# Two attention-only slots, a gate weight spread by a transfer, and loads in another order, in a fused attention and mixture-of-experts kernel

## The chip, the cores and the metric

The kernel runs on one core of one Trainium2 chip. The metric is device time of one execution in microseconds (us), lower is better, taken without the profiler; where a profile is discussed, the span is that of one profiled execution. A run counts as slow when it is more than 1.5% above the fastest run of the same kernel in the same rounds, and only fast runs enter a ratio. In lines of a profile PE is TensorE, PEld its weight loads, DVE VectorE, ACT ScalarE, POOL GpSimd and SP SyncE; L596 is line 596 of that run's kernel. The granted clock is the share of full speed at which TensorE runs.

## The reference

Eight batches of windowed attention, each followed by one expert chosen for the whole batch.

```python
# attention: q, k, v are (8, 8, 576, 64); heads 0-3 a plain window of 32, heads 4-7 a dilated one of 128
scores = np.where(masks, scale * q @ k.T, -1e9)
attn = softmax(scores)                       # exp, row sum, divide
x = (attn @ v).transpose(0, 2, 1, 3).reshape(B, S, 512)
# mixture of experts, w1 (8, 512, 1024), w2 (8, 1024, 512)
logits = x.mean(axis=1) @ w_gate             # one row of 8 logits for each batch
e_idx = argmax(logits)                       # one expert for the whole batch
gate_w = softmax(logits)[e_idx]
out = gate_w * (relu(x @ w1[e_idx]) @ w2[e_idx])
```

Which expert's 2 MB are loaded is known only when the attention of the batch is complete.

## The kernel before

The attention of a batch is cut into four slots of two heads; slots 4b to 4b+3 belong to batch b, 32 slots in all. Queries and keys are transposed on TensorE, a group of two slots at a time and some slots ahead. A slot forms scores, takes the exponent (ScalarE), masks (VectorE), multiplies by v and by ones for the row sums, and normalises by way of a logarithm and an exponent. Between these steps stand items of the feed-forward network of the batch before: 16 of the first layer (four products and a ReLU each), four of the second layer, and a tail. `PIECES` says how many items stand in each slot.

```python
PIECES = [0] * 5 + [6, 3, 4, 4, 1, 1, 2] + [8, 8, 2, 3] * 7

def emit_gate(b):
    lg = ...                                    # gate product, 128x1 against 128x8, 4 chunks
    nc.vector.tensor_copy(out=l_sb[:], in_=lg)
    nc.vector.max_with_indices(mx[:], mi[:], l_sb[:])
    e_val = nc.values_load(mi[0:1, 0:1]..., engines=[ET.Pool], ...)
    # ... three (batch 0: six) loads of w1[e_val] ...
    if b == 0:
        load_1(2, GO[0], "q")                   # second half of batch 2's first group: queries
        load_va(2); load_qb(2); load_w2(e_val, w2b); load_qa(3); load_vb(2)
    else:
        load_vb(b + 2); load_w2(e_val, w2b); load_qa(b + 3)
    load_va(b + 3)
    load_qb(b + 3)

def emit_gate_bc(b):                            # gate weight to 128 partitions
    nc.tensor.matmul(bct[:, 0:1], lhsT=ones1[:], rhs=s["gw"][:], start=True, stop=True)
    nc.vector.tensor_copy(out=gbc[:], in_=bct[:, 0:1])

for t in range(5, len(PIECES)):
    # first half of a slot's items: ReLU on VectorE ("D"), second half on ScalarE ("A")
    # ... run_T (transposes), emit_gate, pre.av_a, cur.sx, pre.av_b, pre.ln, cur.mask, pre.rd,
    #     first half of the items, pre.norm, second half of the items ...
```

`load_qa` and `load_qb` load the queries and keys of a batch's first and second group of slots, `load_va` and `load_vb` the values. All of them and the expert's weights are issued by GpSimd, in program order, into one queue. An item that stands ahead of an attention step in an engine's program can hold it up: in the profile of this kernel VectorE normalised slot 4 at 37.38 us, behind three ReLUs, though ScalarE's reciprocal was ready at 31.76.

The softmax here doesn't subtract the row's maximum and nothing guards it: scores larger than these inputs give would overflow.

## Time and profile before

| | before |
|---|---|
| time, median of 3 | 225.6 us (224.1 to 226.86) |
| profiled span | 220.8 us |
| exponent of slot 4, 12, 31 starts at | 26.5, 67.0, 178.5 us |
| length of a steady batch (four slots) | 23.6 us |
| TensorE busy | 200.8 us, 91% |

I use the start of a slot's exponent on ScalarE as a milestone all through: it is one instruction per slot, easily found, and it stands between that slot's scores and its mask. From slot 4 to 12 is the early part (40.5 us here), from 12 to 31 the steady part (111.5), and after that comes the rest of the feed-forward (42.4). The profile is of a run of 221.91 us. The lines of the profile that carry the argument are shown inside the prediction.

### The profile page before, as it was taken

What the parts mean: (1) busy time and instruction counts of PE and PEld (TensorE: products, weight loads), DVE (VectorE), ACT (ScalarE), POOL (GpSimd) and SP (SyncE); (2) the same over time, 40 slices, a digit from 0 to 9 for tenths busy, and PEclk for the clock granted to TensorE, in tenths of its full rate; (3) what the DMA queues carried; (4) which work ended last, traced back from release to release, by engine and by line L of the source; (5) the groups of instructions that cost most, each with busy time, mean ns of one, the idle gap of its engine ahead of it and who ended that gap; (6) DMA issues with size and microseconds to landing.
All of it is one profiled execution on the core that took longest, in us unless ns stands there. A gap on an engine that the chain in (4) does not pass through costs nothing.

```text
span 220.8 us, 8308 instructions
## 1 busy us (share of the span) xinstructions
PE 200.8 (91%) x3598; PEld 136.0 (62%) x3598; DVE 129.3 (59%) x366; ACT 129.9 (59%) x229; POOL 83.1 (38%) x133
## 2 busy tenths in 40 slices
PE   6976848899889999999999999999999999999992
PEld 1564745675557765777567756776577657747641
DVE  6346644765777756765666766665676556415312
ACT  2368761786767776577656665766667754332320
POOL 7966095614835263525460455236103100500000
PEclk9975556999999999999999999999999999999999
DMA  5999979999999999999999999999995997499523
GB/s 81 182 177 181 97 100 163 207 209 162 207 214 234 216 207 196 245 255 207 199 235 232 213 208 222 219 230 211 218 193 134 190 176 228 50 174 259 117 95 119
DMA packets 49924, 41.18 MB, mean 187 GB/s; under 512 B 23776, under 2 KB 38112, under 8 KB 49888
## 3 DMA queue, kind: packets, MB, share of 16 engines
q0 software_dynamic: 43440, 31.20, 96.4%
q1 hardware_dynamic: 6448, 9.46, 12.7%
q8 instruction: 28, 0.46, 0.8%
q14 instruction: 8, 0.07, 0.1%
HBM read 62.41 MB, written 9.44 MB: 325 GB/s over the span
## 4 chain that ended last, share of the span: by engine, by line
PE 67%; ACT 12%; DVE 9%; DMA 6%; issue 2%; POOL 2%; POOLq 0%; SPq 0%
PE m L622 24%; PE m L602 22%; ACT pt L335 6%; PE nd L370 6%; PE m L637 4%; DMA qm<-in_q_dram 3%; DVE pt L342 3%; PE m L268 3%; DVE xt L507 3%; ACT qk L289 2%; PE m L278 2%; DMA w1b<-in_moe_w_dram 2%; PE ps L302 2%; DVE ht L609 2%; ACT rd L480 2%
## 5 line engine op out<-in xcount | busy, mean ns | idle before, releaser
L602 PE MATMUL m<-xt,w1b 128*128 128x288 bf16 x512 | 69.3, 291 | 5.2 <-DMA w1b<-in_moe_w_dram 3.0
L602 PEld LDWEIGHTS <-w1b 128*128 128x128 bf16 x512 | 49.3, 99 | 21.1 <-issue 4.5
L622 PE MATMUL m<-w2b,ht 128*128 128x512 bf16 x256 | 58.0, 380 | 0.0
L607 ACT ACTIVATE ht<-m 128x288 bf16<-128x288 f32 x63 | 25.8, 409 | 28.8 <-PE m L602 25.3
L622 PEld LDWEIGHTS <-ht 128*128 128x128 bf16 x256 | 23.8, 98 | 27.4
L342 DVE TENSOR_TENSOR pt<-pt,mk 128x896 bf16<-128x896 bf16 x32 | 20.0, 625 | 24.2 <-ACT pt L335 24.2
L507 DVE SCALAR_TENSOR_TENSOR xt<-nd,rd 128x320 bf16<-128x320 f32 (+1 forms) x56 | 28.4, 544 | 7.8 <-ACT rd L480 7.8
L609 DVE TENSOR_SCALAR ht<-m 128x288 bf16<-128x288 f32 x65 | 27.6, 453 | 7.8 <-PE m L602 7.2
L335 ACT ACTIVATE pt<-ps 128x896 bf16<-128x896 f32 x32 | 29.0, 906 | 5.3 <-PE ps L302 5.3
L543 POOL DMA_DIRECT2D w1b<-in_moe_w_dram x9 | 6.4, 708 | 58.9 <-PE m L602 29.6
L289 ACT ACTIVATE qk<-m 128x576 bf16<-128x576 bf16 (+1 forms) x26 | 19.0, 730 | 15.4 <-PE m L268 12.1
L137 POOL DMA_DIRECT2D vm<-in_v_dram x32 | 24.1, 765 | 8.2 <-DMA qm<-in_q_dram 3.0
L286 DVE COPY qk<-m 128x576 bf16<-128x576 bf16 (+1 forms) x26 | 20.4, 783 | 8.4 <-PE m L268 7.1
L480 ACT ACTIVATE rd<-lnd 128x576 f32<-128x576 f32 x32 | 21.8, 683 | 1.0
L370 PEld LDWEIGHTS <-vm 64*64 64x64 bf16 x896 | 15.4, 113 | 9.9 <-issue 3.7
L629 DVE TENSOR_SCALAR osb<-m,gbc 128x512 f32<-128x512 f32 x16 | 12.0, 750 | 15.6 <-PE m L622 15.6
L370 PE MATMUL nd<-pt,vm 64*64 64x64 bf16 (+2 forms) x784 | 18.1, 194 | 3.3 <-DVE negm L575 1.9
L474 ACT ACTIVATE lnd<-nd 128x576 f32<-128x576 f32 x28 | 18.0, 644 | 2.9 <-PE nd L370 2.9
L370 PE MATMUL nd<-pt,ones 64*64 64x256 bf16 (+2 forms) x252 | 16.5, 243 | 0.0
L627 ACT ACTIVATE osb<-m,gbc 128x512 f32<-128x512 f32 x16 | 10.9, 681 | 8.7 <-PE m L622 8.6
L302 PE MATMUL ps<-qk 64*64 64x96 bf16 (+3 forms) x608 | 15.0, 207 | 0.5 <-DVE mx L535 0.4
L302 PEld LDWEIGHTS <-qk 64*64 64x64 bf16 x608 | 14.2, 113 | 1.2 <-issue 0.7
(76 smaller groups left out, 210.5 us busy)
## 6 DMA issues: line engine op xcount, KB each, us to landing
w2b<-in_moe_w_dram POOLq DMA_DIRECT2D x8, 1024.0 KB, 12.6
out_dram<-osb SPq DMA_DIRECT2D x32, 256.0 KB, 6.2
km<-in_k_dram POOLq DMA_DIRECT2D x16, 288.0 KB, 11.9
qm<-in_q_dram POOLq DMA_DIRECT2D x16, 288.0 KB, 12.2
w1b<-in_moe_w_dram POOLq DMA_DIRECT2D x16, 256.0 KB, 10.1
w1b<-in_moe_w_dram POOLq DMA_DIRECT2D x7, 512.0 KB, 10.5
vm<-in_v_dram POOLq DMA_DIRECT2D x8, 256.0 KB, 10.4
vm<-in_v_dram POOLq DMA_DIRECT2D x32, 64.0 KB, 9.4
```

What stands on the lines that cost most here:

```text
L137: nc.gpsimd.dma_start(out=t[:, h], in_=v[b, h, 0:512, :].rearrange("(c p) d -> p c d", p=P))
L289: nc.scalar.activation(out=ev[x][0], in_=ev[x][1], func=AF.Copy)
L302: nc.tensor.matmul(ps[half(e), a, o : o + rhs.free_size()], lhsT=lhsT, rhs=rhs, start=True, stop=True, skip_group_check=True)
L335: nc.scalar.activation(out=pt[:], in_=s["ps"][:, :, 0:NP], func=AF.Exp, scale=0.125)
L342: nc.vector.tensor_tensor(out=pt[:], in0=pt[:], in1=mk[:, g : g + 1, :].to_broadcast([P, 2, NP]), op=ALU.mult)
L370: x = nc.tensor.matmul(oo, lhsT=lhsT, rhs=rhs, start=start, stop=True, skip_group_check=True)
L480: nc.scalar.activation(out=rd[:], in_=s["lnd", n][:], func=AF.Exp, scale=-1.0)
L507: nc.vector.scalar_tensor_tensor(out=o, in0=a0, scalar=1.0, in1=a1, op0=ALU.mult, op1=ALU.mult, accum_out=s["pool"][:, w, c : c + 1],)
L602: nc.tensor.matmul(hm, lhsT=s["w1"][:, c, fc * P : (fc + 1) * P], rhs=s["xt"][:, c, cols], start=(c == 0), stop=(c == 3))
L607: nc.scalar.activation(out=o, in_=hm, func=AF.Relu)
L609: nc.vector.tensor_scalar_max(out=o, in0=hm, scalar1=0.0)
L622: nc.tensor.matmul(om, lhsT=s["ht"][:, fc, r * P : (r + 1) * P], rhs=s["w2"][:, fc, :], start=(fc == 0), stop=(fc == 7))
```

## The change

The intent: slots 5 and 6 do not wait for the first expert's weights, because they hold attention only, with three products on dummy data each, meant to bring TensorE's full clock sooner; the product that spreads the gate weight gives way to a small transfer within the on-chip memory; the gate product moves from the middle of attention to a place beside feed-forward products; in each slot with much feed-forward the first item's product goes ahead of the logarithm, and its ReLU to ScalarE; and loads go in the order of need, with batch 2's queries ahead of the first gate.

```diff
-PIECES = [0] * 5 + [6, 3, 4, 4, 1, 1, 2] + [8, 8, 2, 3] * 7
+PIECES = [0] * 7 + [6, 6, 5, 2, 2] + [8, 8, 2, 3] * 7
...
-    load_1(2, GO[0], "k")
+    load_qk(2, GO[0])
...
-        nc.vector.tensor_copy(out=l_sb[:], in_=lg)
-        nc.vector.max_with_indices(mx[:], mi[:], l_sb[:])
+        nc.vector.max_with_indices(mx[:], mi[:], lg)
+        nc.vector.tensor_copy(out=l_sb[:], in_=lg)
...
-        if b == 0:
-            load_1(2, GO[0], "q")
-            ...
-        load_va(b + 3)
-        load_qb(b + 3)
+        load_va(b + 2)
+        load_qb(b + 2)
+        load_w2(e_val, w2b)
+        load_qa(b + 3)
+        load_vb(b + 2)
...
-        nc.tensor.matmul(bct[:, 0:1], lhsT=ones1[:], rhs=s["gw"][:], start=True, stop=True)
-        nc.vector.tensor_copy(out=gbc[:], in_=bct[:, 0:1])
+        nc.sync.dma_start(out=gbc[:], in_=gw[0:1, 0:1].to_broadcast([1, P]))
...
+        lead = n >= 5 and done % 21 < 16 and pre.on
+            e = "A" if (lead and i == 0) or 2 * i >= n else "D"
+        if gn == 0 and 0 < gb < B:
+            emit_gate(gb)
         if t > 5:
             run_T(t)
-        if gn == 0 and 0 < gb < B:
-            emit_gate(gb)
...
         pre.av_b()
+        if lead:
+            items.pop(0)()
         pre.ln()
...
+        if t in (5, 6):
+            busy_late(3, 512)
```

## The prediction

> **What bounds the kernel now.** I read the busy shares of the page first, then the chain that ended last, then a table of stages, then the timelines of the stages that stood out. The unprofiled time is 225.6 us; the profiled span is 220.8 us.

> From the page (busy time of each engine; the chain by engine and by line; the two DMA queues with packets, MB and share of 16 engines' span):

> ```profile
> PE 200.8 (91%) x3598; PEld 136.0 (62%) x3598; DVE 129.3 (59%) x366; ACT 129.9 (59%) x229; POOL 83.1 (38%) x133
> ...
> PE 67%; ACT 12%; DVE 9%; DMA 6%; issue 2%; POOL 2%; POOLq 0%; SPq 0%
> ...
> q0 software_dynamic: 43440, 31.20, 96.4%
> q1 hardware_dynamic: 6448, 9.46, 12.7%
> ```

> Two resources are nearly full: TensorE (91%, two thirds of the chain) and the transfer engines (the load queue alone 96.4%). So I ask of each stage which of the two is behind. The stage table (from:to and length in us, then busy time and instruction count of PE, weight load, DVE, ACT, POOL, then granted clock, DMA share, GB/s):

> ```profile
> 28.40:33.90 5.50, 2.49 (x92) 2.36 (x92) 1.60 (x5) 3.15 (x6) 5.50 (x9) 0.50 0.91 110
> 33.90:37.40 3.50, 3.48 (x15) 2.24 (x16) 1.31 (x4) 0.00 (x0) 0.80 (x3) 0.51 1.10 170
> 37.40:52.20 14.80, 13.57 (x297) 9.77 (x294) 10.52 (x31) 10.90 (x19) 6.49 (x10) 1.00 1.32 201
> 52.20:65.60 13.40, 11.57 (x281) 7.62 (x282) 9.00 (x24) 10.11 (x16) 7.74 (x12) 1.00 1.22 199
> 65.60:89.25 23.65, 23.32 (x452) 16.17 (x453) 16.02 (x48) 15.99 (x28) 11.34 (x18) 1.00 1.34 217
> 89.25:112.80 23.55, 23.14 (x450) 16.09 (x452) 15.62 (x44) 15.89 (x28) 10.64 (x17) 1.00 1.29 225
> ```

> TensorE idles 5.5-2.49 = 3.0 us in the first row, 1.2 in the third, 1.8 in the fourth, but only 0.33 and 0.41 us in each steady batch of 23.6 us. So the early part has 6 us of holes; later only removing work, or those 0.4 us, can pay.

> The chain in order of time (start, us, what) shows the early hole and one steady batch:

> ```profile
> 28.93 4.86 DMA w1b<-in_moe_w_dram
> 33.92 4.76 PE m L602 x24
> ...
> 95.19 0.68 PE m L268 x36
> 95.87 0.28 PE m L530 x8
> 96.14 0.39 PE nd L370 x19
> ...
> 101.42 0.31 PE m L589 x2
> ...
> 114.29 0.80 ACT pt L335
> 115.11 0.63 DVE pt L342
> 115.73 0.38 DVE ht L609
> 116.15 2.61 PE m L602 x20
> ```

> First pair: TensorE waits for the first expert's w1, behind which slot 5's attention has to queue, since its instructions come after the feed-forward in order. L268, L530, L370: transposes, gate product, attention. L589: the product that spreads the gate weight. The last four: softmax exponent, mask and the first ReLU on VectorE, and only then the next feed-forward product, because its three PSUM banks are full.

> [...] 0.50 is granted up to 37.35 us, 3.4 us after the feed-forward began at 33.92. [...] the gate product in mid attention: from transposes to attention takes 96.14-95.19 = 0.95 us with it and, in the slot before, 0.50 without it (timeline: 112.76 to 113.26), so it costs 0.45 where its own chain piece is 0.28. [...] packets of the load queue run without a break from 35 to 169 us, at about 210 GB/s for weights alone and half of that beside a burst of stores.

> **The change, part by part.**

> *Slots 5 and 6 without feed-forward.* Before, the normalisation of slot 4 could run when its reciprocal was ready (31.76 us) but started at 37.38, behind three ReLUs that waited for w1. After, it runs at once, and slot 6's attention can begin at about 33.1. An attention slot held up by its own chain has a period of 4.2 us (53.3 to 57.5 us in the timeline); with about 0.5 us for half clock slot 7 begins near 37.0 with its transposes. It then has 21 items in 5 slots: 16 of 0.52 (2.61/5), four of 1.78 (chain: 3.56 for two) and a tail of 0.99: 16.5 us. Five slots' own TensorE work is 1.5 each (5.95 us of an eight-item slot less 8 x 0.52 and the 0.3 us stall): 7.5. I add 1.2 for the clock (0 if the dummy products of slots 5 and 6 wake it early[...]) and 0.8 of residual stalls: 37.0+24.0+2.0 = 63.0, and 0.6 for the longer lead of ReLU and logarithm on ScalarE: 63.6, against 65.6. Gain 2.0 us.

> *Gate weight by a transfer.* The product goes from TensorE: 0.31 us, on the chain in each batch. Batch 0's is in the 2.0 above; seven remain: 2.2 us. The transfer is issued three slots before its first use from batch 1 on and two slots before in batch 0, some 10 us; the gate table's 4 KB landed in 4.7 us. It hides. It waits in SyncE's queue for the gate weight, behind which the attention fences stand, but the weight is ready a slot earlier.

> *One ReLU to ScalarE, with its product ahead of the logarithm.* The bank of that item is emptied without waiting for mask or VectorE, so the 0.29 us at 115.86 to 116.15 and its like go. At most the idle time of a batch, 0.4 us, in the five batches that overlap attention fully: 2.0 us.

> *Gate product next to feed-forward.* [...] 0.45-0.28 = 0.17 us, six batches: 1.0 us. The maximum read directly from PSUM brings the expert number about 0.8 us earlier, which only helps loads.

> *Load order.* No bytes change. Query load of batch 2 moves into the gap of 26 to 28.5 us in which the queue was empty: 1.5 us of transfer time won. The rest gives up prefetching 1.77 MB (4.3 us) per batch: w1 lands earlier, batch b+2's second half of keys later. Before, w1 packets of batches 2 to 5 began 23.0 to 23.6 us apart with the engines never idle: transfers can barely go faster than the old TensorE pace. With TensorE at about 22.6 us a batch it catches up. My reckoning of service times (w1 5.0, v 1.6, keys 1.5 us after the queue reaches w1) has the keys just in time in batches 1 to 3 and late by about 0.5 and 0.8 us in 4 and 5. Loss 1.3 us.

> Sum: 2.0+2.2+2.0+1.0-1.3 = 5.9 us; 225.6-5.9 = 219.7 us (2.6%).

> **Rivals.** (a) Transfers become the bound. For: 96.4%, and the never-empty queue. Against: 3.5 us between w1's landing and its use in a steady batch, and 5.0 us for w2 of batch 5. If the smaller prefetch leaves the queue empty at gates or keys late in each batch, gains after the start shrink to about 2 us: 222 to 223.5. (b) The early slots gain nothing: attention alone is bound by its ScalarE-VectorE chain and half clock, and the feed-forward merely moves later: 2 us lost, 221.5. (c) The dummies wake the clock at 37.35 as before and no key is late: 1.2+1.3 more, 217. (d) The spread transfer blocks the fences or lands late: up to 1 us a batch, 226. Against it: the slack above.

> **Range and chances.** (c) gives the low end, (a) the high end; 216.8 to 223.2 should hold it 8 times in 10. 2% is 4.5 us, that is 221.1; my centre is 1.4 us below this, with a spread of about 2.4: faster 0.72, same 0.26, slower 0.02.

> **What would show it.** The first feed-forward product near 39 to 40 us with no wait for w1; granted clock 1.00 from 37.4 (c), 40.8 or 44.2; the transposes of slot 12 near 63.6 instead of 65.6; no spread product in the chain; TensorE idle in a steady batch near 0; batch length about 22.7 instead of 23.6, unless transposes wait for keys, which is (a). If batch length stays at 23.6 the prediction is wrong in its second half; if slot 12 starts at 65 or later, in its first.

## The result, and the profile after

Ratios here and below are the mean time of one kernel's fast runs over that of the other's fast runs of the same rounds, so they are not quite the ratio of the medians quoted beside them.

| | before | after |
|---|---|---|
| first rounds, median | 226.23 us (224.1 to 228.09, 4 runs) | 217.78 us (216.42 to 218.44, 4 runs) |
| ratio, first rounds | | 0.9649, 95% interval 0.9552 to 0.9746: faster |
| later rounds, median | 226.91 us (221.75 to 229.32, 11 runs) | 219.1 us (217.03 to 219.51, 6 runs) |
| ratio, later rounds | | 0.9801, interval 0.9736 to 0.9866: unclear at 2% |
| profiled span | 220.8 us | 214.8 us |
| exponent of slot 4, 12, 31 | 26.5, 67.0, 178.5 us | 25.7, 64.5, 173.1 us |
| steady batches | 23.6, 23.6, 23.6, 23.9 us | 22.5, 22.5, 23.8, 23.1 us |

The medians agree in both rounds (217.78/226.23 = 0.963, 219.1/226.91 = 0.966). The ratios differ because the kernel before scatters: in the later rounds six of its eleven runs, from 226.91 to 229.32, count as slow, and the five fast ones average 223.12. In the first rounds, where the fastest run was 224.1, one of 226.86 still counted as fast. The changed kernel has no such group in ten runs. Among the fast runs of the later, larger rounds the change is worth 2%, in the medians over 3%. Why the kernel before scatters so I did not find out; its one profile is of a fast run. The mean granted clock goes with it (0.936 to 0.947 in its six slow runs of the later rounds, 0.949 to 0.954 in the five fast ones), but no trace shows what lowered it.

Busy times, queues and chain of the changed kernel's page:

```profile
PE 192.6 (90%) x3571; PEld 131.5 (61%) x3588; DVE 122.0 (57%) x343; ACT 133.6 (62%) x243; POOL 83.0 (39%) x133
...
q0 software_dynamic: 43440, 31.20, 97.6%
q1 hardware_dynamic: 7600, 9.46, 14.2%
q8 instruction: 28, 0.46, 0.8%
...
PE 50%; DMA 34%; issue 4%; POOL 4%; DVE 3%; ACT 2%; POOLq 0%; SPq 0%; DVEq 0%
```

The load queue's packets and megabytes are those of before, and its share rose from 96.4 to 97.6%, since the span shrank. The chain that ended last now runs through transfers for a third (6% before). "issue" doubled from 2 to 4%; I had not looked at it. The 28 packets of queue 8 were there before as well, and play a part below.

The stage table of the changed kernel (from:to and length, then busy time and count of PE, weight load, DVE, ACT, POOL, then clock, DMA share, GB/s):

```profile
27.60:32.20 4.60, 4.32 (x103) 3.31 (x103) 2.78 (x9) 3.16 (x6) 4.57 (x9) 0.56 0.95 117
32.20:36.50 4.30, 2.17 (x66) 1.71 (x67) 2.69 (x7) 3.44 (x5) 1.38 (x2) 1.00 1.10 163
...
40.50:47.20 6.70, 4.72 (x125) 3.68 (x124) 3.29 (x11) 4.71 (x9) 1.37 (x2) 1.00 1.24 210
...
63.10:85.60 22.50, 22.39 (x446) 15.79 (x448) 15.05 (x45) 16.52 (x30) 10.10 (x16) 1.00 1.28 221
85.60:108.10 22.50, 22.29 (x448) 15.76 (x450) 14.59 (x41) 16.55 (x30) 9.31 (x15) 1.00 1.29 223
108.10:131.90 23.80, 22.74 (x446) 15.79 (x446) 15.11 (x42) 16.37 (x30) 9.97 (x15) 1.00 1.27 216
```

Four readings. The clock is full from 31.67 us (37.35 before), ahead of the first feed-forward product. The hole before that product has become a hole in slot 7's attention, 4.30-2.17 = 2.1 us. A new hole stands at 40.5 to 47.2: TensorE is idle 2.0 us of 6.7, at full clock. The first two steady batches leave TensorE idle 0.11 and 0.21 us; the next one 1.06.

TensorE's timeline of the changed kernel from 36 us on, lines with long idle time ahead (in brackets: idle before, and what ended it), and the first feed-forward products:

```profile
36.50 0.34 PE L373 MATMUL nd<-pt,vm 64*64 64x64 bf16 x16 [1.97 <-DVE xt L510]
37.41 3.11 PE L596 MATMUL m<-xt,w1b 128*128 128x288 bf16 x24
...
42.91 0.33 PE L373 MATMUL nd<-pt,ones 64*64 64x256 bf16 x6 [1.54 <-issue]
...
49.10 0.23 PE L373 MATMUL nd<-pt,vm 64*64 64x64 bf16 x3 [0.71 <-issue]
...
120.09 0.68 PE L281 MATMUL m<-identb,km 128*128 128x128 bf16 x9 [0.32 <-DMA km<-in_k_dram]
...
131.91 0.69 PE L271 MATMUL m<-ident,km 64*64 64x64 bf16 x32 [0.51 <-DMA km<-in_k_dram]
...
139.26 0.26 PE L305 MATMUL ps<-qk 64*64 64x80 bf16 x6 [0.47 <-issue]
...
167.43 0.27 PE L373 MATMUL nd<-pt,vm 64*64 64x80 bf16 x8 [0.69 <-issue]
```

No wait for w1 is left: the first feed-forward product runs at 37.41. The attention of slot 7 waits 1.97 us for a normalisation, the price of attention alone. Two kinds of wait were not there before: keys that arrive late (120.09, 131.91), and pauses called "issue", in which TensorE waits for nothing that the profile shows. The kernel before has none of these over 0.25 us in its steady part.

The moved ReLU in ScalarE's timeline of the changed kernel (L601 is a ReLU, L477 the logarithm):

```profile
87.76 0.42 ACT L601 ACTIVATE ht<-m 128x288 bf16<-128x288 f32 x1
88.05 0.68 ACT L477 ACTIVATE lnd<-nd 128x576 f32<-128x576 f32 x1
```

And the spread transfer's own view of the changed kernel (issue time in ns; landing time in us, min/median/max):

```profile
L585 SPq DMA_DIRECT2D gbc<-gw x8: 513/524/557, 37.1 to 191.8; - x8
...
DMA to landing us min/median/max: 5.8/7.8/8.8
```

Nothing waited for it; it took 7.8 us, and the first use of its result came 12.5 to 19.9 us after its issue.

By milestones the profiles differ by 0.8 us at slot 4, 2.5 at slot 12, 5.3 at slot 31 and 6.0 at the end. The first 0.8 is luck: slot 4 begins anywhere from 25.4 to 26.9 us in the runs, for kernels alike up to there; why it varies was not tested. That leaves 1.7 for the early part, 2.8 for the steady one and 0.7 for the rest.

### The profile page after: what moved, and what is told of

It reads as the page before. It is cut to its first block, busy times and chain, and to the rows that moved or that the text cites. A ratio compares the mean times of both kernels' runs of the same rounds, so it can differ in the third digit from the quotient of the medians.

```text
span 214.8 us, 8277 instructions
## 1 busy us (share of the span) xinstructions
PE 192.6 (90%) x3571; PEld 131.5 (61%) x3588; DVE 122.0 (57%) x343; ACT 133.6 (62%) x243; POOL 83.0 (39%) x133
## 3 DMA queue, kind: packets, MB, share of 16 engines
q0 software_dynamic: 43440, 31.20, 97.6%
q1 hardware_dynamic: 7600, 9.46, 14.2%
## 4 chain that ended last, share of the span: by engine, by line
PE 50%; DMA 34%; issue 4%; POOL 4%; DVE 3%; ACT 2%; POOLq 0%; SPq 0%; DVEq 0%
DMA qm<-in_q_dram 19%; PE m L596 19%; PE m L616 15%; DMA w2b<-in_moe_w_dram 8%; PE nd L373 5%; DMA km<-in_k_dram 4%; DMA w1b<-in_moe_w_dram 3%; PE m L271 3%; PE ps L305 2%; PE m L631 2%; PE e L373 1%; DVE xt L510 1%; PE m L281 1%; POOL vm L144 1%; POOL km L129 1%
## 5 line engine op out<-in xcount | busy, mean ns | idle before, releaser
L596 PE MATMUL m<-xt,w1b 128*128 128x288 bf16 x512 | 65.7, 287 | 0.0
L616 PE MATMUL m<-w2b,ht 128*128 128x512 bf16 x241 | 57.0, 380 | 0.9 <-issue 0.2
L596 PEld LDWEIGHTS <-w1b 128*128 128x128 bf16 x512 | 48.6, 98 | 13.2 <-issue 0.2
L601 ACT ACTIVATE ht<-m 128x288 bf16<-128x288 f32 x77 | 31.6, 410 | 18.7 <-PE m L596 15.2
L142 POOL DMA_DIRECT2D vm<-in_v_dram x32 | 23.9, 758 | 10.8 <-DMA w1b<-in_moe_w_dram 3.8
L603 DVE TENSOR_SCALAR ht<-m 128x288 bf16<-128x288 f32 x51 | 21.8, 454 | 4.1 <-PE m L596 3.4
L373 PE MATMUL nd<-pt,vm 64*64 64x64 bf16 (+2 forms) x784 | 19.3, 194 | 4.4 <-DVE xt L510 2.0
L373 PE MATMUL nd<-pt,ones 64*64 64x256 bf16 (+2 forms) x252 | 17.0, 243 | 1.5 <-issue 1.5
L477 ACT ACTIVATE lnd<-nd 128x576 f32<-128x576 f32 x28 | 18.1, 646 | 0.0
```

Source lines behind the costliest of these rows:

```text
L142: nc.gpsimd.dma_start(out=t[:, h], in_=v[b, h, 0:512, :].rearrange("(c p) d -> p c d", p=P))
L373: x = nc.tensor.matmul(oo, lhsT=lhsT, rhs=rhs, start=start, stop=True, skip_group_check=True)
L596: nc.tensor.matmul(hm, lhsT=s["w1"][:, c, fc * P : (fc + 1) * P], rhs=s["xt"][:, c, cols], start=(c == 0), stop=(c == 3))
L601: nc.scalar.activation(out=o, in_=hm, func=AF.Relu)
L603: nc.vector.tensor_scalar_max(out=o, in0=hm, scalar1=0.0)
L616: nc.tensor.matmul(om, lhsT=s["ht"][:, fc, r * P : (r + 1) * P], rhs=s["w2"][:, fc, :], start=(fc == 0), stop=(fc == 7))
```

## The experiments

Twelve kernels ran in three groups, each group with its own runs of the kernel before (medians 223.71, 223.73 and 226.91 us). A ratio has an uncertainty of about 1%, 2 us; so where less than that matters I go by milestones and waits in the traces. These come from one profile for each kernel, and two profiles of the same kernel differ, too (see a_same). All results were correct.

### Which part earns the early gain: four kernels

**p_slots**: the kernel before with only the new item counts and the dummy products.

```diff
-PIECES = [0] * 5 + [6, 3, 4, 4, 1, 1, 2] + [8, 8, 2, 3] * 7
+PIECES = [0] * 7 + [6, 6, 5, 2, 2] + [8, 8, 2, 3] * 7
+        if t in (5, 6):
+            busy_late(3, 512)
```

> The kernel before with only slots 5 and 6 freed of feed-forward (new spread of the first 21 pieces, dummy products after both slots). My theory: slot 12's exponent starts about 2 us earlier than the 67.0 us of before, and that is all, so the ratio to before is about 0.991. Rival (the feed-forward only moves later, nothing won): ratio 1.00. Second rival (the dummies wake the clock[...] and this alone is the early gain): half clock ends by 34 us and the gain is 2.5 us or more, ratio 0.989 or less.

Measured: 222.58 us, ratio 0.9992 (0.9902 to 1.0082). TensorE's timeline of p_slots:

```profile
38.24 0.75 PE L283 MATMUL m<-identb,qm 128*128 128x128 bf16 x9 [4.33 <-DMA qm<-in_q_dram]
```

Slot 12 starts at 67.0 us, no earlier than before. My expectation failed. Slot 7 is ready sooner, but in it stand the transpositions of batch 2's queries, which are loaded behind w1, and it now waits for them 4.33 us; from 38.70 us the clock was at half again for 3.4 us.

**p_slotsq**: the same, and batch 2's queries loaded ahead of the first gate.

```diff
-    load_1(2, GO[0], "k")
+    load_qk(2, GO[0])
-            load_1(2, GO[0], "q")
```

> The kernel before with slots 5 and 6 freed of feed-forward, and of the load order only one thing: the query load of batch 2 issued before the gate. The run with the slots alone waited 4.33 us for exactly this load in slot 7. Theory (the slots pay only together with this load): the wait is gone, slot 12's exponent starts near 64.5 instead of 67.0 us, steady batches stay at 23.6 us, ratio to before 0.989. Rival (the early slots are bound elsewhere, so the changed kernel's early gain comes from its other parts): slot 12 stays within 1 us of 67.0, ratio 0.998.

Measured: 221.9 us, ratio 0.9913 (0.9824 to 1.0003). Slot 4 to 12 took 39.6 us, against 40.5 before and 41.6 in p_slots, and the wait for queries is gone. So by these milestones the slots pay only together with this load (the ratio's interval reaches 1). The gain of 0.9 us is less than half of the 2.5 that I had expected (slot 12 started at 66.0 us, not 64.5): two pauses called "issue", 0.93 and 0.76 us, stand in these slots.

**a_oldloads**: the changed kernel with the old load order.

```diff
-    load_qk(2, GO[0])
+    load_1(2, GO[0], "k")
-        load_va(b + 2)
-        ...
+        if b == 0:
+            load_1(2, GO[0], "q")
+            ...
+        load_va(b + 3)
+        load_qb(b + 3)
```

> The changed kernel with the load order of before. My theory: with TensorE at 22.5 us a batch the weights, which come later in this order, would be waited for from about batch 4, in place of the keys; net 0 to 1 us slower than the changed kernel, ratio to before 0.965 to 0.970. Rival (the new order is what lets the steady part run faster): steady batches go back to about 23.5 us, 4 us slower, ratio 0.983. Second rival (the shorter prefetch only costs): no wait for any load in the steady batches, 1 us faster, ratio 0.960.

Measured: 218.68 us, ratio 0.9782 (0.9692 to 0.9872). My expectation, weights that come late from batch 4 on, failed. TensorE's timeline of a_oldloads has the same wait as p_slots:

```profile
38.70 1.14 PE L281 MATMUL m<-identb,qm 128*128 128x128 bf16 x9 [4.53 <-DMA qm<-in_q_dram]
```

Slot 4 to 12 took 41.9 us, 3.1 more than in the changed kernel, with the clock at half from 37.80 to 44.63; slot 12 to 31 took 108.1, no worse than its 108.6. By these milestones the order of loads matters in the early part alone. The times don't show it: 218.68 us lies between the changed kernel's medians, 217.78 and 219.1. The changed kernel with the old order and only batch 2's queries early would tell whether the rest of the new order is worth anything; it wasn't run.

**p_loads**: the kernel before with only the new load order (the reverse of the edit just shown).

> The kernel before with only the new load order, query load of batch 2 before the gate included. Theory (the order pays only together with slots 5 and 6 free of feed-forward, since TensorE was the bound at 23.6 us a batch): slot 12 within 0.7 us of the kernel before, batches 23.5 to 23.8, ratio 0.995 to 1.0. Rival (a) of the prediction (the smaller prefetch slows loads): transpositions wait for keys in each batch, batches above 24 us, ratio above 1.01.

Measured: 228.2 us, ratio 1.0227 (1.0162 to 1.0292): slower by 5 us, where I expected no change. TensorE's timeline of p_loads shows one wait:

```profile
70.33 1.06 PE L268 MATMUL m<-ident,km 64*64 64x64 bf16 x32 [3.64 <-DMA km<-in_k_dram]
```

The transfers of p_loads between 40 and 60 us, in 40 equal slices of 0.5 us (busy share in tenths, then GB/s):

```profile
DMA  9999999999999999999995000000100291091499
GB/s 187 207 209 209 205 211 207 207 211 235 199 210 211 212 203 199 170 153 151 132 73 59 4 0 0 0 0 16 33 0 0 94 389 41 0 57 8 66 197 209
```

The transfer engines run nearly dry for some 6 us from 51 on. In the new order less is prefetched behind a gate, the next gate of this kernel comes only at 54.1 us, and the keys of batch 3's second group, loaded behind it, arrive 3.64 us late. That is rival (a) as the prediction described it, a queue that empties at a gate, but once and not in each batch: the next batches took 23.7, 24.1 and 23.6 us. Slot 4 to 12 took 46.6 us, 6.1 more than before: besides this wait, w1 came 0.75 us later for the first product, and the clock fell to half for 3.4 us at 70.21. In the changed kernel the gate comes at 47.2 us, because the early slots are quicker, and the queue hardly pauses (in its slices of 0.5 us between 40 and 60 us the transfer engines' busy share falls under 8 tenths once, to 5). The empty slots need batch 2's queries early (p_slots, p_slotsq), and the new load order needs the empty slots (p_loads); either one alone gains nothing or loses.

### The gate parts and the ReLU

**p_gate**: the kernel before with the gate product beside feed-forward, the maximum read from PSUM and the spread by a transfer.

```diff
-        nc.tensor.matmul(bct[:, 0:1], lhsT=ones1[:], rhs=s["gw"][:], start=True, stop=True)
-        nc.vector.tensor_copy(out=gbc[:], in_=bct[:, 0:1])
+        nc.sync.dma_start(out=gbc[:], in_=gw[0:1, 0:1].to_broadcast([1, P]))
...
+        if gn == 0 and 0 < gb < B:
+            emit_gate(gb)
         if t > 5:
             run_T(t)
```

> The kernel before with only the gate's parts of the change: spread by a transfer, gate product ahead of the transposes, maximum read from PSUM. My theory: 0.31 us a batch from the spread product (eight of them) and 0.17 us[...] (seven), 3.5 us in all, ratio 0.985; steady batches 0.5 us shorter (23.1 instead of 23.6). Rival (transfers bound the steady part already): steady batches stay at 23.6 and the gain is only the 0.6 us of the last two batches, ratio 0.997.

Measured: 220.91 us, ratio 0.987 (0.9759 to 0.9981), near the 0.985 that I expected, but the rival's 0.997 is inside the interval, too. (The 0.17 us of the expectation is what the gate product cost in mid attention, 0.45, less its own 0.28.) The profiled run was a slow one; of its four steady batches one took the expected 23.1 us, the others 23.4 to 23.8. Its TensorE timeline has a pause of the kind that the changed kernel has, after which TensorE ran slower for a time (two row-sum products of 64x256 in 0.43 us at 67.54, where four took 0.30 at 61.21):

```profile
67.12 0.39 PE L266 MATMUL m<-ident,km 64*64 64x64 bf16 x11 [1.82 <-issue]
```

**a_nolead**: the changed kernel without the moved ReLU.

```diff
-        lead = n >= 5 and done % 21 < 16 and pre.on
+        lead = False
```

> The changed kernel without the product and ReLU drawn ahead of the logarithm (all ReLUs split half and half as before). My theory: the 0.3 us stalls of the first ReLU come back, 0.4 us a batch over five batches, 2.0 us slower than the changed kernel, ratio to before 0.974. Rival (the stall is filled by later work or by waits for keys): less than 0.5 us slower, ratio 0.966.

Measured: 218.37 us, ratio 0.9772 (0.9659 to 0.9884). The stage table of a_nolead, two of its steady batches (columns as above):

```profile
64.70:87.80 23.10, 22.57 (x448) 15.75 (x445) 15.67 (x46) 15.86 (x28) 9.96 (x15) 1.00 1.27 220
87.80:110.90 23.10, 22.49 (x456) 15.75 (x451) 15.37 (x44) 15.77 (x28) 9.96 (x15) 1.00 1.28 223
```

Every batch takes 23.1 us: the two gate parts are worth 23.6-23.1 = 0.5 us a batch, which the prediction had as 0.31+0.17. (a_nolead has the new load order, too; in p_gate, without it, the undisturbed batch took 23.1 as well. How the 0.5 splits between the two parts no run shows.) The stall before a first-layer product is back (0.28 or 0.29 us in four batches), and no key is late. The ReLU takes an undisturbed batch from 23.1 to 22.5. But slot 12 to 31 takes 109.0 us here, and in two profiles of the changed kernel 108.6 and 110.1: over the steady part the ReLU's gain is not to be seen.

### The dummies

**a_nodummy**: the changed kernel without the six dummy products.

```diff
-        if t in (5, 6):
-            busy_late(3, 512)
```

> The changed kernel without the dummy products after slots 5 and 6. Theory (they wake the clock, which came to full at 31.7 us in the profile of the changed kernel): half clock lasts until [...] 40 to 45 us, and slot 12 starts 1 to 2 us later than 64.5; ratio to before 0.972. Rival (the wake-up is due to the denser attention and not to the dummies): full clock before 36 us, slot 12 within 0.5 us, ratio 0.965.

Measured: 218.53 us, ratio 0.9748 (0.9659 to 0.9837). One row of its stage table shows the granted clock (the number after the five engines):

```profile
38.00:44.00 6.00, 5.91 (x82) 4.18 (x83) 2.97 (x8) 2.96 (x5) 4.38 (x7) 0.51 1.26 206
```

The clock stayed at half until 43.93 us, 12.3 us longer, yet slot 4 to 12 took only 1.1 us more (39.9). The two early pauses called "issue" were gone. My reading, an estimate from one profile of each kernel, is that a slower TensorE does not meet them: full clock 12.3 us earlier was worth 1.1 us, and the rest went into waits for something else.

### Late keys and pauses

**a_pieces7**: more feed-forward in slots 7 and 8, to fill the pauses.

```diff
-PIECES = [0] * 7 + [6, 6, 5, 2, 2] + [8, 8, 2, 3] * 7
+PIECES = [0] * 7 + [7, 7, 3, 2, 2] + [8, 8, 2, 3] * 7
```

> The changed kernel with the first 21 pieces spread 7, 7, 3, 2, 2 over slots 7 to 11 instead of 6, 6, 5, 2, 2. In slots 8 and 9 of the changed kernel TensorE stood still for 1.54 and 0.71 us with nothing to wait for; both pauses ended at an instruction whose number is 192 above a multiple of 256, about 1.5 us after a transfer of 16 KB in the instruction queue. Theory (TensorE waits for its next 256 instructions, 6.2 us apart at best under full transfer load): the extra piece (0.52 us) fits into the pause, the products after the pause resume 6.2 us after the boundary before, and the pause shrinks to about 1.0 us; slot 12 starts about 1 us earlier than 64.5, ratio 0.961. Rival (an unseen data dependence): the pause keeps its 1.5 us and moves 0.5 us later, slot 12 unchanged or later, ratio 0.965.

Measured: 218.6 us, ratio 0.9762 (0.9675 to 0.9849). The early pauses shrank from 1.54 and 0.71 to 0.81 and 0.58 us, and the time between their ends stayed at 6.17 us (6.19 in the changed kernel). Slot 4 to 12 gained only 0.3 us, where I had expected 1.

**a_keys**: the second group's keys and queries ahead of its values.

```diff
-        load_va(b + 2)
         load_qb(b + 2)
+        load_va(b + 2)
```

> The changed kernel with batch b+2's second keys and queries loaded ahead of its second values (two load calls swapped). Theory (keys are late in batch 4, as in the profile of the changed kernel: 0.32 and 0.51 us of wait): no transposition waits for a key load in the steady batches, batch 4 shrinks from 23.8 to about 22.8 us, ratio to before 0.960. Rival (transfers as a whole bound those batches): the wait moves to the values or to w1, batch 4 stays above 23.4 us, ratio 0.965.

Measured: 217.14 us, ratio 0.9711 (0.9604 to 0.9817). One wait for keys remained (0.57 us, now those of the first group), and pauses of 0.55 and 0.54 us came at 134 and 140 us. So the batch that was to shrink from 23.8 to 22.8 us (slot 20 to 24) stayed at 23.8, as the rival said. Slot 12 to 31 took 107.9 us.

**a_need**: the second group's keys one gate earlier, ahead of the next w1, and the first group's keys ahead of w2 (shown for batches from 1 on).

```diff
         # behind the loads of w1:
-        load_va(b + 2); load_qb(b + 2); load_w2(e_val, w2b); load_qa(b + 3); load_vb(b + 2)
+        load_half(b + 2, GO[1], "q"); load_va(b + 2); load_half(b + 3, GO[0], "k")
+        load_w2(e_val, w2b)
+        load_half(b + 3, GO[0], "q"); load_vb(b + 2); load_half(b + 3, GO[1], "k")
```

> The changed kernel with the loads of one group reordered by the need that the traces showed: the second half of a batch's keys goes out one gate earlier, before the next w1. Theory (late keys cost what batches 4 and 5 lack): no transposition waits for keys any more (0.3 to 1.0 us before), slot 12 to slot 31 takes about 107.5 us instead of 108.6, ratio about 0.960 to 0.965, w1 not late. Rival (transfers as a whole, data and instructions, are the bound): the wait only moves, to w1 or to pauses called issue, slot 12 to 31 stays at 108.5 to 109, ratio as the changed kernel's.

Measured: 217.65 us, ratio 0.9751 (0.9688 to 0.9813), beside 0.9801 for the changed kernel in the same rounds. TensorE's timeline of a_need from 110 us on has no wait for keys over 0.25 us; what is left in it are pauses:

```profile
133.82 0.17 PE L309 MATMUL ps<-qk 64*64 64x32 bf16 x1 [0.58 <-issue]
...
167.92 0.27 PE L377 MATMUL nd<-pt,vm 64*64 64x80 bf16 x8 [0.70 <-issue]
```

Both theories hold in part. The keys are mended, and slot 12 to 31 took 108.5 us instead of 110.1 in these rounds; the 107.5 that I expected did not come, because the pauses stayed. The mean of six runs is 1.1 us under the changed kernel's, with a standard error of 0.55 worked out from the two spreads: likely the best version, but not shown.

**a_same**: the changed kernel once more (no edit).

> The changed kernel once more, for the spread between runs and as the yardstick of the next three. Ratio to the kernel before 0.965 to 0.972. Its first feed-forward slot begins anywhere between 25.4 and 26.9 us after the start (slot 4's exponents in the runs so far)[...], so about 0.8 us of any single comparison means nothing. If the pauses of TensorE that the profile calls issue come from the supply of instructions in lots of 256, they stand again at the same places of the program, near 43 and 49 us, about 6.2 us apart; if they came from data, they would be tied to data and could vary in their spacing.

Measured: 219.1 us, ratio 0.9801. In the profiled run slot 4 to 12 took 39.0 us and slot 12 to 31 took 110.1, 1.4 us more than in the first profile. The waits over 0.2 us in that part explain it: one of 0.48 for keys and six pauses, together 2.94, so 3.42; in the first profile they are 0.32+0.51+0.21 for keys and 0.47+0.69 in pauses, 2.2. Without them the two have 106.6 and 106.4 us. The first profile was the fastest of the ten runs of this kernel; it flatters it.

### What the pauses are

The pauses end at TensorE instructions whose number, counted from 0 (products, weight loads and the sequencer's own, together), is the same modulo 256. I counted the numbers from the records of traces that lack none of TensorE's (the changed kernel's first trace lacks 17 products, so the 192 in the expectation of a_pieces7 is one off); the third column gives the number and its rest after division by 256:

```
kernel     pause ends at   instruction, mod 256     at what
a_same      44.60 us       1473, 193                row-sum product
a_same      50.52 us       1729, 193                attention product
a_same      89.58 us       3265, 193                scores
a_same      95.87 us       3521, 193                scores
a_same     136.63 us       5057, 193                scores
p_loads     96.49 us       3265, 193                attention product
p_loads    102.68 us       3521, 193                scores
a_shift     57.10 us       1729, 193                transposition
a_shift     75.47 us       2497, 193                feed-forward, layer 1
a_shift     83.30 us       2753, 193                feed-forward, layer 1
a_shift    155.36 us       5569, 193                scores
```

These are examples. Eight such traces (those of p_slotsq, a_nodummy, a_keys, a_pieces7 and a_need beside the three above) have 44 pauses over 0.25 us that end by "issue"; all 44 end at a rest of 193, and 1.25 to 1.59 us after a packet of the queue of kind "instruction" had ended.

**a_shift** tests the estimate: 27 more warm-up products at the start, each with a weight load, move all later work by 54 instructions.

```diff
-    busy(9, 512, 1, 2)
+    busy(36, 128, 1, 2)
```

> The changed kernel with nine warm-up products of 512 columns at the start replaced by 36 of 128 columns: the same columns, 27 products (54 instructions with their weight loads) more on TensorE. Theory (pauses called issue are the end of a lot of 256 instructions whose successor comes late): they move by 54 instructions earlier in the program's work, so the one near 43 us no longer stands before the row-sum product at which it stood, and counted from the first instruction it again falls at about 193 of 256; spacing of two such pauses 6.0 to 6.3 us. Rival (the products there wait for data): the pause stays at the same product. Time as the changed kernel's within 1 us either way.

Measured: 225.74 us, ratio 1.0085 (0.9987 to 1.0183). The pauses moved as the theory says. None stands at the row-sum product any more; those of a_shift stand in other work, at the same numbers. Its TensorE timeline:

```profile
75.47 2.37 PE L596 MATMUL m<-xt,w1b 128*128 128x288 bf16 x18 [0.62 <-issue]
...
83.30 2.87 PE L596 MATMUL m<-xt,w1b 128*128 128x288 bf16 x22 [2.33 <-issue]
```

The rival, data, is out: these are ordinary first-layer products in the middle of a group. One part of my expectation failed, the time. The warm-up lines of the changed kernel and of a_shift, one fence for each, tell why:

```profile
1.59 5.73 PE L95 MATMUL e<-warm 128*128 128x512 bf16 x9 [1.59 <-DVE warm L79]
```

```profile
1.59 11.49 PE L95 MATMUL e<-warm 128*128 128x128 bf16 x36 [1.59 <-DVE warm L79]
```

A dummy of 512 columns took 0.64 us, one of 128 took 0.32, not a quarter; as an estimate from these two widths, (0.64-0.32)/384 = 0.83 ns a column plus 0.21 us each. The edit held up the start by 11.49-5.73 = 5.8 us, and the mean of its fast runs was 225.03 us against 218.68 for a_same, 6.3 us longer, so it tells of places, not of time. The spacing of 6.0 to 6.3 us that I named failed for one pair, too (75.47 to 83.30 is 7.8 us: that packet began only at 81.04, 5.6 us after the first of the two).

## Why the prediction was right or wrong

The time is right: 219.7 us was predicted, the medians were 217.78 and 219.1, both inside 216.8 to 223.2, and faster by 2% was the likeliest outcome. As a gain, 5.9 us was predicted; the means of the fast runs differ by 7.9 us in the first rounds and by 4.4 in the later ones. Its steps fared differently.

*Slots 5 and 6: right in size, with a condition that the prediction did not see as one.* 2.0 us were predicted, 1.7 measured (1.4 in the second profile). That the sum came out is partly luck. Slot 7's transposes began at 33.87 us, not near 37.0, and slot 12's at 62.99, so that the five slots took 29.1 us instead of 26.6 (24.0 of work, 2.6 for clock, stalls and a longer lead). The work is as reckoned, TensorE busy for 24.3; but it stood idle for 4.9, of which 1.97 are the wait for a normalisation and 2.25 the pauses. One error hid the other. The prediction credits the query load of batch 2 with transfer time alone; it is in truth what lets slot 7 go on, and without it the step is worth nothing (p_slots; a_oldloads waits 4.53 us). Rival (b), no early gain, is what p_slots shows.

*The clock: rival (c) came true in half.* The allowance of 1.2 us for a late clock was not needed: full clock came at 31.67 us, before the feed-forward began and earlier than any time that the prediction named. (It did not always last: in a_nolead the clock was at half again from 37.90 to 41.31.) But its worth went to the two pauses at 42.91 and 49.10, 2.25 us that no step of the prediction had. a_nodummy, at half clock up to 43.93, loses 1.1 us and has no such pauses.

*Spread product and gate product: right.* 0.31+0.17 = 0.48 us a batch predicted, 0.5 measured (a_nolead). Behind slot 31, where two spread products went, 0.7 us was won in the first profile (42.4 to 41.6) and 0.5 in the second. Rival (d) did not come: nobody waits for the transfer. (The 0.50 us without the gate product that the prediction reads at 112.76 to 113.26 is from slot 20; "the slot before" is the one before the next gate, not before the one at 95.19.)

*The ReLU: the mechanism is right, its yield was given back.* 0.4 us a batch predicted, 0.6 measured in an undisturbed batch. Over slots 12 to 31 nothing is left of it: 109.0 us without, 108.6 and 110.1 with. TensorE reaches each need sooner, and stands there: 1.04 us for keys and 1.16 us in pauses in the first profile.

*Late keys: right in kind, mis-sized as the whole loss.* 0.5 and 0.8 us were predicted for the second-group keys loaded at the gates of batches 4 and 5. The first profile has 0.51 for the one (at 131.91 us), 0.21 for the other (at 155.05), and 0.32 for keys of a first group (at 120.09): 1.04 in all. What the sum lacks is the term for the pauses: 1.16 us in slots 12 to 31 in the first profile, 2.94 in the second. So the step that was wrong is "transfers can barely go faster than the old TensorE pace" taken for data only. The packets of the instruction queue are counted on the same 16 engines (0.8% of their span, beside 97.6% for the load queue), and in a_same two of them began only 3.7 and 4.0 us after a boundary. And the earlier expert number, which "only helps loads", helped none in the steady part: it was ready 0.66 us after the gate product starts instead of 0.95, 0.3 us sooner and not 0.8; but for batches 2 to 5 the first load of w1 was issued 3.3 to 5.1 us after the gate product, 2.4 before. Each time it went out 0.3 to 0.6 us after w2 of the batch before, the load eight places earlier, had landed (at 71.68, 94.62, 118.03 and 141.57 us; w1 went out at 71.97, 95.23, 118.65 and 142.19), so I read it as GpSimd waiting for that load; the profile names other releasers there (VectorE's mask and ReLUs).

As a sum, for slots 12 to 31: 111.5 before; without waits 106.4 and 106.6, so 4.8 to 5.0 won; 2.2 and 3.4 of that given back.

*Rival (a)* holds for no kernel with the empty slots, and for p_loads once, with a wait of 3.64 us in a kernel slower by 5.

Why this kernel meets the pauses and the old one hardly did is an estimate: a batch has about 894 TensorE instructions (446 products and 448 weight loads), 3.5 lots of 256, at 6.2 us (the stretches above) 21.7 us. The batch took 23.6 us before and takes 22.5 now. By this estimate packets keep up on average and fall behind in places; that the many short products of attention make such places is a guess, which no run tested. Whether fewer instructions would remove the pauses, or another order of loads, was not tried; the two orders tried (a_keys, a_need) left them.

## What to carry to other kernels

Parts of a change can depend on each other both ways: the empty slots and the load order, each alone, gained nothing or lost 5 us, and together they gave the early gain; one load, batch 2's queries, was the link that showed in the traces. Here a faster TensorE beside a load queue at 97.6% met keys that came up to 0.51 us late and pauses at fixed places of its instruction stream, 1.16 and 2.94 us of them in the steady part of two profiles: so look at the idle time called "issue" as well as at waits for data before predicting. One profile of a kernel that scatters by 2 us is not enough to tell a step of half a microsecond: two profiles of the same kernel differed by 1.4 us in the same nineteen slots.
